# Fewer routed slots, and the high and low halves of the activations side by side in one matmul

## The chip, the cores and the metric

The kernel runs on one core of a Trainium2 chip. The metric is the device time of one execution in microseconds (us). Five things work side by side: TensorE (PE; its weight loads are PEld in the profile), VectorE (DVE), ScalarE (ACT), GpSimd (POOL) and the DMA queues, here mainly SyncE's (SP). Each engine takes its instructions in the order in which the program issued them to it.

## The reference

Three layers on 1,536 tokens of width 512, all in float32: a linear attention with decay, a dense mixture of 4 experts, and a routed mixture of 8 experts. The change lies in the third:

```python
logits = x @ w_gate                      # 1536 x 8
expert_idx = np.argmax(logits, axis=1)   # one expert per token
gate_w = probs[np.arange(N), expert_idx]
for e in range(8):
    xe = x[expert_idx == e]              # n_e x 512
    h = np.maximum(xe @ w1[e], 0.0)      # 512 x 1024
    out[expert_idx == e] = gate_w[...] * (h @ w2[e])   # 1024 x 512
```

With the reference's inputs the experts get 161, 102, 158, 127, 272, 269, 247 and 200 tokens.

## The kernel before, in words

Every float32 matrix is split into a high part (rounded to float32r by ScalarE) and a low part (the rest, by VectorE). A product is three float32r matmuls into one PSUM accumulator: high weight with high activation, high weight with low activation, low weight with high activation (`mm3`, L330).

The routed layer begins at 613 us of the span. Eight experts run one after the other; each has a fixed number of slots (`CAPS`): expert 0 has its own, the other seven are sorted by their token count on the chip and take `BY_RANK` in the order of `TURNS`. So the turns 0 to 7 have 256, 288, 128, 288, 256, 256, 256 and 128 slots. Tokens beyond a capacity would go through a slow loop at the end (`tc.If`, L1014), which does not run with these inputs.

One expert has two products. The first (`moe2_mm1`, L859) makes the hidden layer in 8 groups f of 128 rows, each a PSUM accumulator `g` of 128 x slots over 4 chunks d; ScalarE takes the relu into the high part, VectorE makes the low part (`relu_split`, L339). The second comes in two forms. With at most 256 slots (`moe2_mm2_rows`, L901) the hidden activations are the stationary operand and 512 columns of the weights stream past them: 48 matmuls of 512 columns for 256 slots. With 288 slots (`moe2_mm2`, L930) the weights are stationary and the slots stream: 4 groups m, an eviction `yt`, and transposes back (`moe2_out`, L943). A turn of 128 slots uses the row form for both products. The last step multiplies by the gate and scatters rows to the output.

Between the matmul groups stand hooks (L970 to L990), and through these the order of work on ScalarE and VectorE is set. `hook1`, after each group of the first product, splits two pieces of the same expert's second weights (`split_to`, L138: a ScalarE cast and a VectorE subtraction of 128 x 512 each; a weight half is 4 pieces, an expert has 16). `hook2`, four times in the second product, transposes the next expert's rows (`rows_T`, L846) and splits the next expert's first weights; after a turn in row form it also splits three pieces of its second weights ahead. The matmul accumulators rotate through three PSUM buffers (`ps_mm`). In expert 0, `route_order` and `route_rest` put small VectorE instructions at the start and into the first `hook2`.

Of the kernel before, what the change touches and what calls it, by code (L numbers as in the profile page):

```python
# [8 lines left out]
F32 = mybir.dt.float32  # L9
F32R = mybir.dt.float32r  # L10
BF16 = mybir.dt.bfloat16
I32 = mybir.dt.int32
AF = mybir.ActivationFunctionType
ALU = mybir.AluOpType
# [4 lines left out]
P = 128  # L19
# [7 lines left out]
KD = DM // P  # L27
# [3 lines left out]
FC = HF // P  # L31
# [1 line left out]

BY_RANK = [288, 288, 256, 256, 256, 128, 128]
TURNS = [0, 5, 1, 2, 3, 4, 6]
CAPS = [256] + [BY_RANK[i] for i in TURNS]
NSS = [-(-c // P) for c in CAPS]
STS = [c // n for c, n in zip(CAPS, NSS)]  # L40
CAP, ST, NS = CAPS[0], STS[0], NSS[0]
MOST, NMOST = max(CAPS), max(NSS)
W = DM + 2
FAR = 1 << 20
OMAX = (N - min(CAPS[0], BY_RANK[0]) + P - 1) // P
# [4 lines left out]
def body(ctx: ExitStack, tc: tile.TileContext, lam, att, dp, w1a, w2a, wg, wgt, w1b, w2b, out):  # L50
    nc = tc.nc
    V, A, G, T, SP = nc.vector, nc.scalar, nc.gpsimd, nc.tensor, nc.sync
# [277 lines left out]
    def mm3(ps, parts, first, last):  # L330

        n = 3 * len(parts)
        i = 0
        for (lh, ll), (rh, rl) in parts:
            for l, r in ((lh, rh), (lh, rl), (ll, rh)):
                T.matmul(ps, l, r, start=first and i == 0, stop=last and i == n - 1)  # L336
                i += 1

    def relu_split(ps, tag, n, nm, pl, bufs, most=None):  # L339
        hh, hl = (  # L340
            pl.tile([P, most or n], F32R, tag=tag + x, name=nm + x, bufs=bufs)[:, :n]
            for x in "hl"
        )
        A.activation(out=hh, in_=ps, func=AF.Relu)  # L344
        V.scalar_tensor_tensor(  # L345
            out=hl, in0=ps, scalar=0.0, in1=hh.bitcast(F32), op0=ALU.max, op1=ALU.subtract
        )
        return hh, hl
# [273 lines left out]
    with tc.manual_schedule():  # L622
# [15 lines left out]
            out=upper, in_=upper, compare_op=ALU.is_ge, fill=1.0, base=0,  # L638
# [150 lines left out]
        y, z = NC - 2, NC - 1  # L789
# [17 lines left out]
        gx = z_ctx.enter_context(pool("gx", 2))  # L807

        def rows_tiles(e):
            return tuple(  # L810
                gx.tile([P, KD, MOST], F32R, tag="xg" + x, name=f"xg{x}{e}")[:, :, :CAPS[e]]
                for x in "hl"
            )

        def rows_split(hi, lo, ps):
            A.copy(out=hi, in_=ps)
# [2 lines left out]
        xg = {0: rows_tiles(0)}  # L819
# [4 lines left out]
        gp = z_ctx.enter_context(pool("gp", 2))  # L824
# [21 lines left out]
        def rows_T(e, s):  # L846
            if e >= E2:
                return
            if s == 0:
                xg[e] = rows_tiles(e)  # L850
            hi, lo = xg[e]
            st = STS[e]
            tr = ps_tr.tile([P, KD, P], F32, tag="tr", name=f"xt{e}_{s}")[:, :, :st]
            for d in range(KD):
                T.transpose(tr[:, d, :], xb_t[e][:st, s, d * P:d * P + P], ident[:st, :st])
            c = slice(s * st, s * st + st)
            rows_split(hi[:, :, c], lo[:, :, c], tr)

        def moe2_mm1(e, f):  # L859
            hi, lo = xg[e]  # L860
            k, c = 2 * (E1 + e) + f // FC, (f % FC) * P
            wh, wl = wt[0, k]
            n = CAPS[e]
            ps = ps_mm.tile([P, 512], F32, tag="mm", name=f"g{e}_{f}")
            mm3(
                ps[:, :n],
                [((wh[:, d, c:c + P], wl[:, d, c:c + P]), (hi[:, d, :], lo[:, d, :]))
                 for d in range(KD)],
                True, True,
            )  # L870
            return relu_split(ps[:, :n], "g", n, f"g{e}_{f}", gp, 2 * FC + 2, MOST)


        def moe2_mm1_rows(e, h, hook):
            hi, lo = xg[e]
            wh, wl = wt[0, 2 * (E1 + e) + h]
            n = CAPS[e]
            ps = ps_mm.tile([P, 512], F32, tag="mm", name=f"gr{e}_{h}")
            for d in range(KD):
                mm3(ps[:n], [((hi[:, d, :], lo[:, d, :]), (wh[:, d, :], wl[:, d, :]))],  # L880
                    d == 0, d == KD - 1)
                if d < KD - 1:
                    hook(h * KD + d)
            g = gp.tile([P, HF], F32, tag="gr", name=f"gr{e}_{h}")
            A.activation(out=g[:n], in_=ps[:n], func=AF.Relu)
            hook(h * KD + KD - 1)
            return g
# [13 lines left out]
        def moe2_mm2_rows(e, hs, y, hook):  # L901
            st, ns, xb = STS[e], NSS[e], xb_t[e]
            step = FC * ns // 2
            ps = [
                ps_mm.tile([P, 512], F32, tag="mm", name=f"zr{e}_{s}") for s in range(ns)
            ]
            i = 0
            for h in range(2):
                wh, wl = wt[1, 2 * (E1 + e) + h]
                for s in range(ns):  # L910
                    for f in range(FC):
                        hh, hl = hs[h * FC + f]
                        c = slice(s * st, s * st + st)
                        mm3(ps[s][:st], [((hh[:, c], hl[:, c]), (wh[:, f, :], wl[:, f, :]))],
                            h == 0 and f == 0, h == 1 and f == FC - 1)
                        i += 1
                        if i % step == 0 and i < 4 * step:
                            hook(i // step - 1)
                    if h == 0:
                        continue  # L920
                    gate = xb[:st, s, DM:DM + 1]
                    V.tensor_scalar(  # L922
                        out=y[:st, s, :], in0=ps[s][:st], scalar1=gate, scalar2=None,
                        op0=ALU.mult,
                    )
                    scatter(out, xb.bitcast(I32)[:st, s, DM + 1:W], y[:st, s, :], N, "out")
            hook(3)


        def moe2_mm2(e, hs, m):  # L930
            n = CAPS[e]
            ps = ps_mm.tile([P, 512], F32, tag="mm", name=f"z{e}_{m}")
            c = slice(m * P, m * P + P)
            parts = []
            for f, (hh, hl) in enumerate(hs):
                wh, wl = wt[1, 2 * (E1 + e) + f // FC]
                parts.append(((wh[:, f % FC, c], wl[:, f % FC, c]), (hh, hl)))
            mm3(ps[:, :n], parts, True, True)
            yt = gp.tile([P, MOST], F32, tag="yt", name=f"yt{e}_{m}", bufs=3)
            A.copy(out=yt[:, :n], in_=ps[:, :n])  # L940
            return yt

        def moe2_out(e, yt, m, y):  # L943
# [19 lines left out]
        for e in range(E2):  # L963
            k = 2 * (E1 + e)
            load_rows(e + 2)
            y = gp.tile([P, NMOST, DM], F32, tag="y", name=f"y{e}")
            hs = []
            turns = []

            def hook1(i):  # L970
                if late:
                    late.pop()()
                split_to(1, k + 1, 2)
                if i == KD + 1 and turns:
                    hs.extend(turns.pop()())

            def hook2(i):
                if turns:
                    hs.extend(turns.pop()())
                if late:  # L980
                    late.pop()()
                if e == 0 and i == 0:
                    route_rest()
                if e + 1 < E2:
                    if i < NSS[e + 1]:
                        rows_T(e + 1, i)
                    if CAPS[e] <= 2 * P and i > 1:
                        split_to(1, k + 2, 3)
                    else:
                        split_to(0, k + 3, 2 if i == 0 else 3)  # L990

            if CAPS[e] <= P:
                for h in range(2):
                    g = moe2_mm1_rows(e, h, hook1)
                    turns.append(lambda h=h, g=g: moe2_turn(e, h, g))
            else:
                for f in range(2 * FC):
                    hs.append(moe2_mm1(e, f))
                    hook1(f)
            if CAPS[e] <= 2 * P:  # L1000
                moe2_mm2_rows(e, hs, y, hook2)
            else:
                for m in range(KD):
                    yt = moe2_mm2(e, hs, m)
                    hook2(m)
                    late.append(lambda e=e, yt=yt, m=m, y=y: moe2_out(e, yt, m, y))
# [7 lines left out]
    with tc.If(n_r > 0):  # L1014
        with pool("op", 1) as op:
# [12 lines left out]
                out=upto, in0=tiles_e, scalar1=float(P), scalar2=None, op0=ALU.mult  # L1028
            )
            V.tensor_copy(out=base, in_=upto)  # L1030
            for e in range(1, E2):
                V.tensor_tensor(
                    out=upto[:, e:e + 1], in0=upto[:, e:e + 1], in1=upto[:, e - 1:e], op=ALU.add
# [4 lines left out]
                out=pick, in0=desc.unsqueeze(1).to_broadcast([P, NC, E2]),  # L1038
                in1=m2_all.unsqueeze(2).to_broadcast([P, NC, E2]), op=ALU.is_equal,
            )  # L1040
            V.tensor_tensor(
                out=own_t, in0=pick, in1=base.unsqueeze(1).to_broadcast([P, NC, E2]), op=ALU.mult
# [129 lines left out]
```

## Time and profile before

| | |
|---|---|
| time, median of 3 runs | 797.97 us (796.89 to 798.29) |
| the profiled execution's own time | 797.57 us |
| its span, first to last instruction | 795.6 us |
| granted TensorE clock, mean | 0.996 |
| busy share of the span: PE, PEld, DVE, ACT, POOL | 98%, 82%, 46%, 27%, 15% |
| routed layer | from about 613 us on |

The profiled execution is 0.40 us below the median, and its span 2.0 us below its time. A busy share is an average over stages: VectorE's tenths in the slices of the page go from 2 in the dense layer to 7 in the routed one.

### The profile page before, as it was taken

Reading aid. Unit: us, or ns where it says so; the run is one execution under the profiler, and the core shown is the slowest. Engines: PE = TensorE matmul, PEld = TensorE weight load, DVE = VectorE, ACT = ScalarE, POOL = GpSimd, SP = SyncE. Lnnn points to the kernel's source line nnn. Section 1 sums busy time; section 2 is a strip of 40 time slices with the busy share of each in tenths; the row PEclk is TensorE's granted clock in tenths of the full one; section 3 lists DMA queues with packets and bytes.
Section 4 is the critical chain, followed back from the end, with each engine's and each line's share of the span. In section 5 each row is a group of like instructions: output and inputs, shape, how many; then the busy total and the mean of one; then the engine's idle time right before and its main releaser. Section 6 shows DMA issues by size and latency. Waiting matters only on the chain. (4 is left out here: it accounts for less than half of the span.)

```text
span 795.6 us, 11255 instructions
## 1 busy us (share of the span) xinstructions
PE 778.1 (98%) x4472; PEld 651.5 (82%) x4472; DVE 365.1 (46%) x800; ACT 217.4 (27%) x438; POOL 116.4 (15%) x117
## 2 busy tenths in 40 slices
PE   7899999999999999999999999999999999999996
PEld 6787778888888888888888888878898898998884
DVE  5443321332322232233223233588886757677553
ACT  3222222110121221111022121011134546555552
POOL 4553200100110110001011010011122013121101
PEclk9999999999999999999999999999999999999999
DMA  8654264110010001011001002000123767766550
GB/s 304 228 165 155 80 228 144 53 54 1 26 54 28 26 27 54 0 54 47 7 27 54 26 27 80 0 27 14 41 80 134 280 206 240 277 210 219 176 200 28
DMA packets 24375, 81.20 MB, mean 102 GB/s; under 512 B 3132, under 2 KB 4156, under 8 KB 24192
## 3 DMA queue, kind: packets, MB, share of 16 engines
q1 hardware_dynamic: 22032, 74.14, 27.6%
q0 software_dynamic: 2144, 6.31, 2.0%
q8 instruction: 36, 0.59, 0.3%
q14 instruction: 19, 0.16, 0.1%
q10 hardware_dynamic: 144, 0.01, 0.0%
HBM read 69.40 MB, written 11.70 MB: 102 GB/s over the span
## 5 line engine op out<-in xcount | busy, mean ns | idle before, releaser
L336 PE MATMUL h<-xh,w0h 128*128 128x512 f32 (+1 forms) x432 | 162.9, 377 | 1.1 <-ACT xh L298 1.1
L336 PE MATMUL h<-xl,w0h 128*128 128x512 f32 (+1 forms) x432 | 159.3, 369 | 0.9 <-DVE xl L299 0.8
L336 PE MATMUL h<-xh,w0l 128*128 128x512 f32 (+1 forms) x432 | 159.5, 369 | 0.0
L378 DVE SCALAR_TENSOR_TENSOR acc<-y,p_sb,acc 128x512 f32<-128x512 f32 x84 | 63.1, 751 | 124.6 <-PE y L336 122.8
L336 PEld LDWEIGHTS h<-xh,w0h 128*128 128x128 f32 x432 | 81.2, 188 | 17.1 <-ACT xh L298 1.8
L336 PEld LDWEIGHTS h<-xl,w0h 128*128 128x128 f32 x432 | 81.2, 188 | 17.0 <-DVE xl L299 2.1
L336 PEld LDWEIGHTS h<-xh,w0l 128*128 128x128 f32 x432 | 81.1, 188 | 16.0
L344 ACT ACTIVATE ht_0h<-h 128x512 fp32r<-128x512 f32 (+1 forms) x27 | 14.9, 551 | 246.4 <-PE h L336 246.4
L161 POOL TENSOR_TENSOR w0l<-raw,w0h 128x512 fp32r<-128x512 f32 x17 | 22.3, 1316 | 251.6 <-ACT w0h L159 251.6
L159 ACT CAST w0h<-raw 128x512 fp32r<-128x512 f32 x96 | 53.9, 619 | 7.3 <-DMA raw<-in_w1a 7.3
L336 PE MATMUL g<-xgl,w0h 128*128 128x256 f32 (+1 forms) x192 | 55.0, 287 | 0.4 <-DVE xgl L817 0.4
L336 PE MATMUL g<-xgh,w0h 128*128 128x256 f32 (+1 forms) x192 | 54.9, 286 | 0.2 <-issue 0.2
L336 PE MATMUL g<-xgh,w0l 128*128 128x256 f32 (+1 forms) x192 | 55.1, 287 | 0.0
L159 ACT CAST w1h<-raw 128x512 fp32r<-128x512 f32 x96 | 54.3, 618 | 1.5 <-PE zr L336 1.5
L161 DVE TENSOR_TENSOR w1l<-raw,w1h 128x512 fp32r<-128x512 f32 x80 | 52.5, 694 | 0.3 <-ACT w1h L159 0.3
L161 DVE TENSOR_TENSOR w0l<-raw,w0h 128x512 fp32r<-128x512 f32 x79 | 51.2, 691 | 0.4
L96 POOL DMA_INDIRECT out<-y,xb x16 | 24.6, 1540 | 152.2 <-DVE y L922 75.8
L345 DVE SCALAR_TENSOR_TENSOR ht_0l<-h,ht_0h 128x512 fp32r<-128x512 f32 (+1 forms) x27 | 17.1, 632 | 60.1 <-ACT ht_0h L344 60.1
L336 PE MATMUL y<-w1h,ht_0h 128*128 128x512 f32 x96 | 39.4, 410 | 0.0
L430 DVE CUSTOM_DVE_ANT_0 jl<-acc,wgb 128x512 f32<-128x512 f32 x56 | 38.4, 685 | 0.8
L336 PE MATMUL y<-w1h,ht_3h 128*128 128x512 f32 x96 | 38.2, 397 | 0.0
L336 PE MATMUL y<-w1h,ht_1l 128*128 128x512 f32 x96 | 38.1, 397 | 0.0
(283 smaller groups left out, 1431.0 us busy)
## 6 DMA issues: line engine op xcount, KB each, us to landing
raw<-in_w1b SPq DMA_DIRECT2D x32, 512.0 KB, 6.8
raw<-in_w2b SPq DMA_DIRECT2D x32, 512.0 KB, 3.2
att<-in_att SPq DMA_DIRECT2D x24, 512.0 KB, 4.3
raw<-in_w1a SPq DMA_DIRECT2D x16, 512.0 KB, 7.6
raw<-in_w2a SPq DMA_DIRECT2D x16, 512.0 KB, 3.9
bins<-fill SPq DMA_DIRECT2D x1, 4626.0 KB, 21.7
xb<-bins SPq DMA_DIRECT2D x4, 514.0 KB, 6.3
wgb<-in_wgt SPq DMA_DIRECT2D x1, 2048.0 KB
```

The lines of the kernel that those rows point to most:

```text
L96: i = G.indirect_dma_start(out=dst, out_offset=bass.IndirectOffsetOnAxis(ap=idx, axis=0), in_=src, in_offset=None, bounds_check=rows - 1, ...
L159: A.copy(out=hi, in_=t)
L161: (G if i < 3 else V if i >= 4 * ROUTED else los[i % 2]).tensor_tensor(out=lo, in0=t, in1=hi.bitcast(F32), op=ALU.subtract)
L336: T.matmul(ps, l, r, start=first and i == 0, stop=last and i == n - 1)
L344: A.activation(out=hh, in_=ps, func=AF.Relu)
L345: V.scalar_tensor_tensor(out=hl, in0=ps, scalar=0.0, in1=hh.bitcast(F32), op0=ALU.max, op1=ALU.subtract)
L378: V.scalar_tensor_tensor(out=acc[:, t, 0:DM], in0=ps, scalar=p_sb[:, t, e:e + 1], in1=acc[:, t, 0:DM], op0=ALU.mult, op1=ALU.add,)
L430: V.tensor_tensor_reduce(out=jl, in0=acc[:, t, 0:DM], in1=rt["wgb"][:, e, :], scale=1.0, scalar=0.0, op0=ALU.mult, op1=ALU.add, accum_out= ...
```

## The change

The capacities of the turns become 176, 288, 128, 288, 256, 208, 160 and 128, 1,632 slots in all for 1,856. A turn whose capacity is a multiple of 128 keeps the row form (turns 2, 4, 7). A turn between 128 and 256 slots is now "wide" (turns 0, 5 and 6): high and low activations lie side by side in one tile, one matmul of the high weight takes both (2n columns, for n slots), and one of the low weight takes the high half (n columns). The accumulator then has two halves; ScalarE copies the second to SBUF, VectorE adds the first to it, and relu, low part and transposes read the sum in SBUF. Wide turns use the weights-stationary form for the second product too. In the row form the gate multiplication moves from VectorE to ScalarE.

```diff
-BY_RANK = [288, 288, 256, 256, 256, 128, 128]
+BY_RANK = [288, 288, 256, 208, 160, 128, 128]
-CAPS = [256] + [BY_RANK[i] for i in TURNS]
+CAPS = [176] + [BY_RANK[i] for i in TURNS]
+BY_ROWS = [c % P == 0 for c in CAPS]
+WIDE = [P < c < 2 * P for c in CAPS]
...
         def rows_tiles(e):
-            return tuple(
-                gx.tile([P, KD, MOST], F32R, tag="xg" + x, name=f"xg{x}{e}")[:, :, :CAPS[e]]
-                for x in "hl"
-            )
+            n = CAPS[e]
+            both = gx.tile([P, KD, 2 * MOST], F32R, tag="xg", name=f"xg{e}")[:, :, :2 * n]
+            return both[:, :, :n], both[:, :, n:], both
...
+        def product(e, ps, parts):
+            n = CAPS[e]
+            if not WIDE[e]:
+                mm3(ps[:, :n], [(w, x[:2]) for w, x in parts], True, True)
+                return ps[:, :n]
+            for i, ((wh, wl), (hi, _, both)) in enumerate(parts):
+                T.matmul(ps[:, :2 * n], wh, both, start=i == 0, stop=False)
+                T.matmul(ps[:, :n], wl, hi, start=False, stop=i == len(parts) - 1)
+            s = gp.tile([P, MOST], F32, tag="yt", name=f"s{ps.name}", bufs=4)[:, :n]
+            A.copy(out=s, in_=ps[:, n:2 * n])
+            V.tensor_tensor(out=s, in0=ps[:, :n], in1=s, op=ALU.add)
+            return s
...
         def moe2_mm1(e, f):
...
-            return relu_split(ps[:, :n], "g", n, f"g{e}_{f}", gp, 2 * FC + 2, MOST)
+            g = gp.tile([P, 2 * MOST], F32R, tag="g", name=f"g{e}_{f}", bufs=2 * FC + 2)
+            hh, hl = g[:, :n], g[:, n:2 * n]
+            A.activation(out=hh, in_=s, func=AF.Relu)
+            V.scalar_tensor_tensor(
+                out=hl, in0=s, scalar=0.0, in1=hh.bitcast(F32), op0=ALU.max,
+                op1=ALU.subtract,
+            )
+            return hh, hl, g[:, :2 * n]
...
         def moe2_mm2_rows(e, hs, y, hook):
-                    V.tensor_scalar(
-                        out=y[:st, s, :], in0=ps[s][:st], scalar1=gate, scalar2=None,
-                        op0=ALU.mult,
-                    )
+                    A.activation(out=y[:st, s, :], in_=ps[s][:st], func=AF.Copy, scale=gate)
...
         def moe2_mm2(e, hs, m):
-            mm3(ps[:, :n], parts, True, True)
-            yt = gp.tile([P, MOST], F32, tag="yt", name=f"yt{e}_{m}", bufs=3)
-            A.copy(out=yt[:, :n], in_=ps[:, :n])
+            s = product(e, ps, parts)
+            if WIDE[e]:
+                return s
+            yt = gp.tile([P, MOST], F32, tag="yt", name=f"yt{e}_{m}", bufs=4)
+            A.copy(out=yt[:, :n], in_=s)
...
-                    if CAPS[e] <= 2 * P and i > 1:
+                    if BY_ROWS[e] and i > 1:
                         split_to(1, k + 2, 3)
...
-            if CAPS[e] <= 2 * P:
+            if BY_ROWS[e]:
                 moe2_mm2_rows(e, hs, y, hook2)
```

## Rows read from the trace of the kernel before

**Rows 1.** The page, busy time of each engine over the span.

```profile
PE 778.1 (98%) x4472; PEld 651.5 (82%) x4472; DVE 365.1 (46%) x800; ACT 217.4 (27%) x438; POOL 116.4 (15%) x117
```

**Rows 2.** Busy time by stretch: first product of turn 0; turns 0, 5, 6.

```profile
core 0: us, PE busy (x) PEld busy (x) DVE busy (x) ACT busy (x) POOL busy (x), PEclk, DMA share, GB/s
613.00:624.40 11.40, 11.40 (x96) 11.40 (x97) 9.70 (x26) 7.08 (x17) 0.00 (x0) 1.00 0.70 230
...
613.00:636.70 23.70, 23.70 (x156) 21.45 (x157) 17.96 (x46) 13.64 (x31) 0.00 (x0) 1.00 0.70 247
...
729.20:752.60 23.40, 23.40 (x154) 21.20 (x153) 15.42 (x29) 12.54 (x26) 2.20 (x2) 1.00 0.59 213
752.60:775.50 22.90, 22.90 (x149) 20.77 (x148) 14.93 (x28) 12.48 (x26) 3.16 (x3) 1.00 0.59 202
```

**Rows 3.** Timeline of PE: start us, us, instruction, count, idle before.

```profile
607.57 0.96 PE L451 MATMUL lg<-wg_sb,xt 128*128 128x8 f32 x8
608.38 0.38 PE L616 MATMUL warm_rt<-ones 128*128 128x128 bf16 x4
...
624.49 0.39 PE L336 MATMUL zr<-w1h,g_0h 128*128 128x512 f32 x1
...
627.04 0.40 PE L336 MATMUL zr<-w1h,g_3l 128*128 128x512 f32 x1
...
656.17 0.49 PE L947 MATMUL yo<-ident,yt 128*96 128x128 f32 x3
656.42 0.38 PE L336 MATMUL z<-g_0h,w1h 128*128 128x288 f32 x1
```

**Rows 4.** Timeline of ACT and DVE, first product of turn 0.

```profile
616.41 1.13 ACT L159 CAST w1h<-raw 128x512 fp32r<-128x512 f32 x2
...
621.83 0.39 ACT L344 ACTIVATE g_5h<-g 128x256 fp32r<-128x256 f32 x1 [1.04 <-PE g L336]
...
617.07 0.42 DVE L345 SCALAR_TENSOR_TENSOR g_1l<-g,g_1h 128x256 fp32r<-128x256 f32 x1
617.41 1.28 DVE L161 TENSOR_TENSOR w1l<-raw,w1h 128x512 fp32r<-128x512 f32 x2
618.61 0.42 DVE L345 SCALAR_TENSOR_TENSOR g_2l<-g,g_2h 128x256 fp32r<-128x256 f32 x1
...
622.25 0.42 DVE L345 SCALAR_TENSOR_TENSOR g_5l<-g,g_5h 128x256 fp32r<-128x256 f32 x1 [0.16 <-ACT g_5h L344]
```

**Rows 5.** Timeline of DVE and ACT: a hand-over from DVE to ACT.

```profile
609.79 0.22 DVE L465 TENSOR_SCALAR df<-lg,mx 128x8 f32<-128x8 f32 x1
...
610.10 0.21 ACT L484 ACTIVATE ex<-df 128x8 f32<-128x8 f32 x1 [2.44 <-DVE df L465]
```

**Rows 6.** Groups by line and shape, ACT and DVE: count, busy us, mean ns.

```profile
L159 ACT CAST w1h<-raw 128x512 fp32r<-128x512 f32 x56 | 31.4, 618 | 1.5 <-PE zr L336 1.5
...
L816 ACT CAST xgh<-xt 128x512 fp32r<-128x512 f32 x8 | 4.7, 587 | 12.1 <-PE xt L855 12.1
...
L161 DVE TENSOR_TENSOR w1l<-raw,w1h 128x512 fp32r<-128x512 f32 x64 | 40.5, 681 | 0.0
...
L817 DVE TENSOR_TENSOR xgl<-xt,xgh 128x512 fp32r<-128x512 f32 x8 | 5.5, 692 | 18.8 <-ACT xgh L816 18.8
```

**Rows 7.** Timeline of DVE: end of `route_order`, start and end of `route_rest`.

```profile
615.44 0.17 DVE L586 TENSOR_SCALAR nth<-who 128x7 int32<-128x7 f32 x1
...
625.44 0.20 DVE L594 TENSOR_TENSOR tmp<-place,places 128x49 f32<-128x49 f32 x1
...
627.11 0.16 DVE L611 CAST tiles_n<-count 128x1 int32<-128x1 f32 x1
```

**Rows 8.** Busy time by stretch, with the granted clock (PEclk), columns as in Rows 2.

```profile
5.00:10.00 5.00, 3.28 (x44) 2.65 (x46) 4.39 (x12) 0.23 (x1) 0.00 (x0) 1.00 1.03 370
10.00:15.00 5.00, 4.23 (x36) 3.20 (x32) 2.49 (x5) 3.02 (x6) 4.12 (x4) 0.66 1.03 383
...
608.00:610.00 2.00, 0.84 (x12) 0.71 (x12) 1.83 (x11) 0.00 (x0) 1.26 (x2) 1.00 0.00 0
```

More of the change, by code (lines that the diff above doesn't have):

```diff
@@ L337, in mm3, with relu_split @@
                 i += 1
-    def relu_split(ps, tag, n, nm, pl, bufs, most=None):
+    def relu_split(ps, tag, n, nm, pl, bufs):
         hh, hl = (
-            pl.tile([P, most or n], F32R, tag=tag + x, name=nm + x, bufs=bufs)[:, :n]
+            pl.tile([P, n], F32R, tag=tag + x, name=nm + x, bufs=bufs)
             for x in "hl"
@@ L850, in rows_T @@
                 xg[e] = rows_tiles(e)
-            hi, lo = xg[e]
+            hi, lo, _ = xg[e]
             st = STS[e]
@@ L857, in rows_T @@
             rows_split(hi[:, :, c], lo[:, :, c], tr)
+        def product(e, ps, parts):
[10 more added lines that the diff above has]
+            return s
         def moe2_mm1(e, f):
-            hi, lo = xg[e]
+            hi, lo, both = xg[e]
             k, c = 2 * (E1 + e) + f // FC, (f % FC) * P
@@ L864, in moe2_mm1 @@
             ps = ps_mm.tile([P, 512], F32, tag="mm", name=f"g{e}_{f}")
[L865 to L869, printed above, removed]
+            s = product(e, ps, [
+                ((wh[:, d, c:c + P], wl[:, d, c:c + P]),
+                 (hi[:, d, :], lo[:, d, :], both[:, d, :])) for d in range(KD)
+            ])
+            g = gp.tile([P, 2 * MOST], F32R, tag="g", name=f"g{e}_{f}", bufs=2 * FC + 2)
[4 more added lines that the diff above has]
+                op1=ALU.subtract,
             )
-            return relu_split(ps[:, :n], "g", n, f"g{e}_{f}", gp, 2 * FC + 2, MOST)
+            return hh, hl, g[:, :2 * n]
         def moe2_mm1_rows(e, h, hook):
-            hi, lo = xg[e]
+            hi, lo, _ = xg[e]
             wh, wl = wt[0, 2 * (E1 + e) + h]
@@ L911, in moe2_mm2_rows @@
                     for f in range(FC):
-                        hh, hl = hs[h * FC + f]
+                        hh, hl = hs[h * FC + f][:2]
                         c = slice(s * st, s * st + st)
@@ L934, in moe2_mm2 @@
             parts = []
-            for f, (hh, hl) in enumerate(hs):
+            for f, h in enumerate(hs):
                 wh, wl = wt[1, 2 * (E1 + e) + f // FC]
-                parts.append(((wh[:, f % FC, c], wl[:, f % FC, c]), (hh, hl)))
-            mm3(ps[:, :n], parts, True, True)
-            yt = gp.tile([P, MOST], F32, tag="yt", name=f"yt{e}_{m}", bufs=3)
-            A.copy(out=yt[:, :n], in_=ps[:, :n])
+                parts.append(((wh[:, f % FC, c], wl[:, f % FC, c]), h))
+            s = product(e, ps, parts)
[3 more added lines that the diff above has]
+            A.copy(out=yt[:, :n], in_=s)
             return yt
```

## The prediction

> **What bounds the kernel now.** First the page: TensorE is busy 98% of the span, no other engine half as much [rows 1]. The change lies in the routed layer, so the stretches of that layer come next. In turn 0 the first product has 96 matmuls of 256 columns in 11.40 us, 0.119 us each, and TensorE and its weight loads are both busy all the time; VectorE has 9.70 us of work there and ScalarE 7.08 [rows 2]. So TensorE sets the pace, but VectorE stands close behind. The timelines show how an eviction goes: relu on ScalarE ends at 621.83 + 0.39 = 622.22, VectorE's low part starts at 622.25 [rows 4], and nothing goes back. The last view to keep is VectorE's rhythm where two weight pieces follow each group: low parts start at 617.07 and 618.61, 1.54 us apart, against 11.40/8 = 1.43 us per group on TensorE [rows 2, 4]. Today this lag is absorbed, since only the first four of the eight groups carry pieces.
>
> **What TensorE saves.** 48 matmuls of 512 columns: 624.49 to 627.04 is 11 steps, 0.232 us each [rows 3]. Between 256 and 512 columns that is 0.441 ns a column, so 320, 352 and 416 columns cost 0.147, 0.161 and 0.190 us. A float32r matmul of 160 to 208 columns is not in the trace. Its lower end is 0.232 us scaled by columns, 0.073 to 0.094; its upper end the 0.119 of 256 columns. The eight gate matmuls stream only 8 columns behind full weight loads and start 0.81/8 = 0.101 us apart [rows 3]; I take that, as a weight load alone must cost about as much. A pair is then 0.262 us for 176 slots, 0.291 for 208, 0.248 for 160; a group of four pairs (first product) 1.05, 1.16, 0.99 us; of eight pairs (second product) 2.10, 2.33, 1.98. New are eight transposes back a turn: three take 0.25 us [rows 3], two 0.17, of which three pairs lie inside a turn, 0.5 us. If TensorE alone counted, turn 0 would fall from 23.7 us to 64 x 0.262 plus 1.2 (what the present 23.7 leaves after 11.4 and 48 x 0.232: row transposes, joins) plus 0.5 = 18.5 us.
>
> **What the eviction now costs.** Per group there were two steps, ScalarE then VectorE. Now there are four: ScalarE copies, VectorE adds, ScalarE takes the relu, VectorE the low part, and both engines keep program order, so VectorE stands still between add and low part. Prices: VectorE's two-operand step is 0.42 us at 256 columns [rows 4] and 0.692 at 512 [rows 6], so 0.34 at 176, 0.37 at 208, 0.32 at 160, and the next one starts 0.08 before its end (617.41 against 617.49). ScalarE from PSUM is 0.39 at 256 [rows 4] and 0.587 at 512 [rows 6], so 0.33 at 176, 0.35 and 0.32; from SBUF I add the 0.618 - 0.587 = 0.03 [rows 6], for the relu now reads SBUF; the next starts 0.10 earlier than its end. The hand-over to VectorE is 0.03 [rows 4]; that to ScalarE is at most 0.09 (610.01 to 610.10 [rows 5]) and at least, I assume, the same 0.03; I take 0.06, halfway. The add itself is not in the trace; I price it as the low part, which has the same two operands, with 0.08 either way.
>
> [...]
>
> From one add to the next, with no weight pieces, 176 slots: 0.34 + 0.06 + 0.36 + 0.03 + 0.26 = 1.05 us, just TensorE's pace. With two pieces: the relu starts 0.40 after the add, the first cast 0.66, it ends at 1.28 (0.618), its subtraction starts at 1.31, the second 0.60 later [rows 4], the next add at 2.51. So 2.5 us a group against TensorE's 1.05. For 208 slots 2.56 (one piece 1.96, none 1.13), for 160 slots 2.48 and 1.00. An accumulator is free after its add, so with three of them group f + 3 waits for add f.
>
> **Turn 0**, from a start that lies 0.5 us earlier (612.5: the selections, the placing matmuls and the first evictions are 176 columns wide and no longer 256; 16 x 0.018 plus some 0.2 of VectorE and ScalarE). VectorE is busy with `route_order` until 615.6 [rows 7], now 615.1: add 0. Eight pieces follow groups 0 to 3, so add 4 is at 615.1 + 4 x 2.5 = 625.1, TensorE begins group 7 at 625.5 and ends the first product at 626.55: 14.05 us, not 11.4. Low part 7 is ready at 625.1 + 3 x 1.05 + 1.1 = 629.3; only then can the second product's first accumulator be finished, 629.6. Three groups of 2.1, 1.2 and 0.5 lead to 637.6. That is 25.1 us for 23.7: +1.4.
>
> **Turn 1** waits for VectorE. After 630.4 it has, before the third part of turn 1's columns, three adds (0.8), `route_rest` (625.44 to 627.27, 1.85 [rows 7]), three low parts of rows (1.5), five subtractions (3.0) and two gate multiplications (0.7): 638.3 instead of 637.6, and 0.5 more at the next transposes, which wait for add 3. +1.3.
>
> **Turn 5** (208) follows a row turn that has split three pieces ahead. Those and the gate step, now ScalarE's, put add 0 at 2.9 us (0.43 to the eviction, 0.5, three casts 1.56, copy 0.35). Add 3 is 2.56 + 2.56 + 1.96 later, at 10.0; groups 6 and 7 end at 12.8; low part 7 is ready at 15.7, the first accumulator done at 16.0, then 3 x 2.33 + 0.8 + 0.5 = 24.3 us for 23.4 [rows 2]: +0.9.
>
> **Turn 6** (160) has eight pieces again, because a wide turn before it splits none ahead. Add 0 at 1.7, add 4 at 11.6, first product 13.0, first accumulator 16.0, then 3 x 1.98 + 0.4 + 0.5 = 22.8 for 22.9 [rows 2]: -0.1.
>
> **Turn 7** meets the same late VectorE as turn 1, which today it does not: +1.2. Turns 2, 3 and 4 stay. At the end ScalarE's gate step is 0.15 shorter than VectorE's.
>
> Sum: -0.5 + 1.4 + 1.3 + 0.9 - 0.1 + 1.2 - 0.15 = +4.05 us. On the profiled execution's 797.57 that is 801.6, and with its distance of 0.4 to the median 802.0. Its own bounds: hand-overs of 0.03 or 0.09 give +3 or +5; the add 0.08 shorter or longer, over 36 evictions, -2.5 or +2.5; the narrow matmul at its ends -0.1 or +0.6, since TensorE waits anyway. The forecast alone is 800 to 806.
>
> What I cost at nothing: the weight loads. Each turn still needs 4.2 MB, the queue runs 6 loads of 0.5 MB ahead, and 213 to 247 GB/s over turns 0 and 5 [rows 2] suffice today; turns do not get shorter here, so no more is asked. If they did (18.5 us), it would be 4.7 MB with the rows, 254 GB/s, about today's rate. The wider tiles take the room of the two they replace.
>
> **The rivals.**
>
> A, faster: the exchange hides. If VectorE never waited in it, a group with two pieces would take its own work alone, 0.26 + 0.26 + 1.20 = 1.72 us. Then turns 0, 5 and 6 gain 3.1, 1.9 and 3.0, and the lag that turns 1 and 7 inherit (2.5) goes: 4.05 - 10.5 = -6.5, 791.5 us. For it speaks that four groups of each first product carry no pieces, so that lag can be made up; against it that ScalarE's relu is ordered behind the add and ahead of the casts. It decides from 2.2 us a group: there the sum is zero. In the extreme, TensorE alone counts: 18.5 us for turn 0, 19.9 and 16.8 for turns 5 and 6, 782 us. VectorE's own 8 x 0.52 + 8 x 0.60 = 9.0 us against TensorE's 8.4 in the first product excludes most of that. [...] I give it 0.04 of A's chance.
>
> B, the narrow matmul is dear. At twice 0.232 us scaled, 0.145 to 0.19 us each, TensorE's group comes to 1.2 to 1.5 us and its second product sets more of the time: about +7, 805 us. Nothing in the trace shows a float32r matmul so narrow.
>
> [...]
>
> D, a capacity is exceeded. The counts fit (127 tokens for 128 slots, 158 for 160 are the tightest); one more would start the slow loop, with four loads of 1 MB. 1 in 100.
>
> **How the numbers follow.** The forecast 0.54; A 0.21; B, C and D 0.10 together; between A and the forecast, within 0.2% (1.6 us, about what a measurement can tell from no change), 0.15. Slower 0.64, same 0.15, faster 0.21. The range 793 to 809 leaves out A's lower half, 0.10, and the worst of B and C, 0.07.
>
> **What would show it.** Right: TensorE idle some 1.4 us before groups 4 to 7 of turns 0 and 6, ended by VectorE's add; adds 2.5 us apart while pieces are split and 1.05 after; first products of 13 to 14 us; turn 1's first matmul waiting for its columns. Wrong: adds under 2.2 us apart, or first products under 11.4 us. [...]

## The result and the profile after

| | before | changed |
|---|---|---|
| time, median of 6 runs | 797.19 us | 805.18 us (802.58 to 807.66) |
| ratio, with 95% interval | | 1.0098 [1.008, 1.0116] |
| profiled execution, span | 797.57, 795.6 us | 805.12, 803.3 us |
| granted clock, mean | 0.996 | 0.984 |

The change makes the kernel 8 us slower; the forecast was 4 us slower (802.0, range 793 to 809). The six runs differ more than those of before, and with their clock: the fastest, 802.58 us, had 0.992, the slowest, 807.66, had 0.982.

The page's lines for busy time and clock (answer to [rows 1]):

```profile
PE 778.1 (97%) x4448; PEld 654.7 (81%) x4448; DVE 371.4 (46%) x838; ACT 227.4 (28%) x478; POOL 120.6 (15%) x117
...
PEclk9999999999999999999999999999998899999988
```

There are fewer slots, yet TensorE is busy as long as before. The clock line says where to look: it dips twice in the routed layer, which had no such dip before. By the start of each turn's first matmul in the timeline of TensorE, in us:

| | forecast | before | changed | difference |
|---|---|---|---|---|
| start of turn 0 | -0.5 | 612.98 | 613.71 | +0.7 |
| turn 0 | +1.4 | 23.7 | 26.3 | +2.5 |
| turn 1 | +1.3 | 26.7 | 27.9 | +1.2 |
| turns 2, 3, 4 | 0 | 65.75 | 65.95 | +0.2 |
| turn 5 | +0.9 | 23.4 | 24.7 | +1.3 |
| turn 6 | -0.1 | 22.95 | 23.7 | +0.8 |
| turn 7, to its last matmul | +1.2 | 11.9 | 12.9 | +1.0 |

These make 7.7 us, the difference of the spans. One execution's start of turn 0 also moves with what lies before it: with the full clock at the entry it was 612.0 us in one kept trace (e2_order) and 613.13 in another (e3_clock). The changed kernel's busy time in the same turns (answer to [rows 2]; columns as there):

```profile
613.70:640.00 26.30, 24.11 (x149) 23.38 (x148) 19.55 (x55) 15.56 (x40) 0.00 (x0) 0.81 0.56 192
...
733.80:758.50 24.70, 21.59 (x144) 20.31 (x142) 17.63 (x39) 15.54 (x38) 1.19 (x2) 1.00 0.57 198
758.50:782.20 23.70, 21.11 (x142) 20.29 (x140) 17.29 (x41) 14.48 (x37) 3.33 (x2) 0.86 0.58 186
```

TensorE now has gaps in all three wide turns, and in turns 0 and 6 its clock is at 0.81 and 0.86 on average. What ends its gaps stands in its timeline:

```profile
621.78 0.43 PE L868 MATMUL g<-xg,w0h 128*128 128x352 f32 x1 [0.90 <-DVE sg L872]
622.05 0.24 PE L869 MATMUL g<-xg,w0l 128*128 128x176 f32 x1
622.13 0.35 PE L868 MATMUL g<-xg,w0h 128*128 128x352 f32 x1
...
622.40 0.35 PE L868 MATMUL g<-xg,w0h 128*128 128x352 f32 x1
...
626.72 0.66 PE L868 MATMUL g<-xg,w0h 128*128 128x352 f32 x1
...
628.85 0.56 PE L868 MATMUL z<-g,w1h 128*128 128x352 f32 x1
...
642.30 0.42 PE L967 MATMUL yo<-ident,sz 128*88 128x128 f32 x2 [0.33 <-DVE sz L872]
...
742.55 0.46 PE L868 MATMUL g<-xg,w0h 128*128 128x416 f32 x1 [1.08 <-DVE sg L872]
...
765.41 0.41 PE L868 MATMUL g<-xg,w0h 128*128 128x320 f32 x1 [1.18 <-DVE sg L872]
```

`sg`, line 872, is the add. The long waits stand before groups 5 and 6 in turns 0 and 6 (4 and 5 in turn 5), not before each of groups 4 to 7 as the forecast's sign had it. A pair of 352 and 176 columns takes 622.40 - 622.13 = 0.27 us (0.262 forecast). The eviction in the timelines of DVE and ACT (answer to [rows 4]):

```profile
618.92 0.34 DVE L872 TENSOR_TENSOR sg<-g,sg 128x176 f32<-128x176 f32 x1
619.67 0.34 DVE L888 SCALAR_TENSOR_TENSOR g<-sg,g 128x176 fp32r<-128x176 f32 x1 [0.42 <-ACT g L887]
620.18 1.29 DVE L165 TENSOR_TENSOR w1l<-raw,w1h 128x512 fp32r<-128x512 f32 x2 [0.17 <-ACT w1h L163]
621.39 0.33 DVE L872 TENSOR_TENSOR sg<-g,sg 128x176 f32<-128x176 f32 x1
...
626.33 0.33 DVE L872 TENSOR_TENSOR sg<-g,sg 128x176 f32<-128x176 f32 x1
...
627.34 0.33 DVE L872 TENSOR_TENSOR sg<-g,sg 128x176 f32<-128x176 f32 x1
628.09 0.34 DVE L888 SCALAR_TENSOR_TENSOR g<-sg,g 128x176 fp32r<-128x176 f32 x1 [0.42 <-ACT g L887]
628.35 0.33 DVE L872 TENSOR_TENSOR sg<-g,sg 128x176 f32<-128x176 f32 x1
...
619.29 0.35 ACT L887 ACTIVATE g<-sg 128x176 fp32r<-128x176 f32 x1 [0.89 <-DVE sg L872]
```

Add to add with two pieces: 621.39 - 618.92 = 2.47 us; without: 1.01. VectorE stands 0.42 us between add and low part and 0.17 before the first subtraction; ScalarE waits 0.89 for the add. And the clock by stretch (answer to [rows 8]):

```profile
610.00:617.00 7.00, 7.00 (x34) 6.89 (x32) 4.26 (x22) 1.73 (x7) 0.97 (x1) 0.51 0.34 115
617.00:624.00 7.00, 5.21 (x37) 4.79 (x36) 5.47 (x12) 4.57 (x12) 0.00 (x0) 0.98 0.85 250
624.00:630.40 6.40, 6.00 (x23) 5.70 (x23) 4.11 (x12) 3.67 (x11) 0.00 (x0) 0.50 0.90 365
...
767.00:774.00 7.00, 5.91 (x23) 5.65 (x24) 4.75 (x13) 3.55 (x11) 0.00 (x0) 0.51 0.71 246
```

In three stretches of some 7 us the granted clock was 0.50 to 0.51 (half clock below). One lies at the entry, where the placing matmuls took 0.214 us each: 613.41 - 610.41 is 14 steps. They began 0.43 us earlier than before and ended later, so the start of turn 0 loses its time in them. The two others begin in the first products of turns 0 and 6, after the waits had begun. The placing matmuls in the changed kernel, and the first of them before:

```profile
610.10 0.52 PE L558 MATMUL px<-sel,ah 128*128 128x176 f32 x1
610.41 0.42 PE L558 MATMUL px<-sel,al 128*128 128x176 f32 x1
...
613.41 0.41 PE L558 MATMUL px<-sel,al 128*128 128x176 f32 x1
...
610.53 0.39 PE L554 MATMUL px<-sel,ah 128*128 128x256 f32 x1
```

### The profile page after: what moved, and what is told of

Its sections match the earlier page's. It is cut to its first block, busy times and chain, and to the rows that moved or that the text cites. A ratio compares the mean times of both kernels' runs of the same rounds, so it can differ in the third digit from the quotient of the medians.

```text
span 803.3 us, 11286 instructions
## 1 busy us (share of the span) xinstructions
PE 778.1 (97%) x4448; PEld 654.7 (81%) x4448; DVE 371.4 (46%) x838; ACT 227.4 (28%) x478; POOL 120.6 (15%) x117
## 4 chain that ended last, share of the span: by engine, by line
PE 83%; issue 5%; DVE 5%; DMA 2%; ACT 2%; POOL 1%; SPq 0%; POOLq 0%; ACTq 0%; DVEq 0%
PE h L340 33%; PE y L340 33%; PE g L340 4%; PE z L340 3%; DVE w1l L165 2%; PE zr L340 2%; PE qk L238 1%; PE xo L297 1%; PE xo L291 1%; DVE w0l L165 1%; DMA raw<-in_w1a 1%; ACT w1h L163 1%; PE z L868 1%; DMA xe<-bins 1%; DMA raw<-in_w1b 1%
## 5 line engine op out<-in xcount | busy, mean ns | idle before, releaser
L100 POOL DMA_INDIRECT out<-y,xb x16 | 29.4, 1841 | 155.6 <-DVE y L969 94.2
L868 PE MATMUL g<-xg,w0h 128*128 128x352 f32 (+2 forms) x96 | 33.9, 415 | 7.4 <-DVE sg L872 7.3
L340 PE MATMUL g<-xg,w0h 128*128 128x288 f32 (+1 forms) x192 | 38.0, 292 | 0.4 <-DVE xg L820 0.4
L165 POOL TENSOR_TENSOR w1l<-raw,w1h 128x512 fp32r<-128x512 f32 x16 | 21.1, 1322 | 114.7 <-ACT w1h L163 114.7
```

What stands on the lines that cost most here:

```text
L100: i = G.indirect_dma_start(out=dst, out_offset=bass.IndirectOffsetOnAxis(ap=idx, axis=0), in_=src, in_offset=None, bounds_check=rows - 1, ...
L165: (G if i < 3 else V if i >= 4 * ROUTED else los[i % 2]).tensor_tensor(out=lo, in0=t, in1=hi.bitcast(F32), op=ALU.subtract)
L868: T.matmul(ps[:, :2 * n], wh, both, start=i == 0, stop=False)
```

## The experiments

Two theories were to be told apart and sized: the exchange between ScalarE and VectorE, in program order, holds the wide turns; and TensorE's clock, 0.50 to 0.51 in the three stretches above, adds the rest. Rivals: the work that the added copies and adds bring; narrow matmuls. Each line of the table is a median and the ratio to the kernel before in the same comparison, with its 95% interval; the ratio is taken over the runs and is not exactly that of the two medians.

| | time, us | ratio |
|---|---|---|
| e1_plain: three narrow matmuls, two-step eviction | 819.73 | 1.0274 [1.0257, 1.0291] |
| e2_order: weight pieces between add and relu | 792.95 | 0.9954 [0.9937, 0.9971] |
| e3_clock: TensorE kept busy at the entry and in the waits | 801.25 | 1.0046 [1.0033, 1.006] |
| e4_wide256: wide turns with the old capacities | 817.26 | 1.0243 [1.0228, 1.0259] |
| e5_plain_up: e1 with TensorE kept busy at the entry | 796.05 | 0.9984 [0.9975, 0.9994] |
| e6_even: e2, one piece a group, busy at the entry | 789.19 | 0.99 [0.9884, 0.9917] |
| e7_order_up: e2, busy at the entry | 793.3 | 0.995 [0.9933, 0.9966] |
| e8_up: the changed kernel, busy at the entry | 803.38 | 1.0088 [1.0067, 1.0109] |

**e2_order.** The same instructions in another order.

```diff
-                    hs.append(moe2_mm1(e, f))
-                    hook1(f)
+                    hs.append(moe2_mm1(e, f, hook1))
...
             hh, hl = g[:, :n], g[:, n:2 * n]
+            if WIDE[e]:
+                hook(f)
             A.activation(out=hh, in_=s, func=AF.Relu)
```

(Turns that are not wide call the hook after the low part, as before.)

> The changed kernel with one order turned round: in a wide turn the two weight pieces come between the add and the relu, no longer behind the low part. The same instructions, the same data. Theory (VectorE's and ScalarE's waits for each other in program order are the cost): a group with two pieces takes VectorE's own work, 1.72 us instead of 2.47, first products of turns 0 and 6 fall by about 3 us, turn 5 by 1.9, 797 in all (8 less). Rival (it is the amount of work that the added copies and adds bring): adds stay 2.4 to 2.5 us apart, 804 to 806.

It is 12.2 us faster than the changed kernel and 4.7 faster than the kernel before (797.63 in the same comparison). VectorE's timeline in turn 0:

```profile
616.00 0.33 DVE L872 TENSOR_TENSOR sg<-g,sg 128x176 f32<-128x176 f32 x1
616.25 1.28 DVE L165 TENSOR_TENSOR w1l<-raw,w1h 128x512 fp32r<-128x512 f32 x2
617.46 0.33 DVE L890 SCALAR_TENSOR_TENSOR g<-sg,g 128x176 fp32r<-128x176 f32 x1
617.71 0.33 DVE L872 TENSOR_TENSOR sg<-g,sg 128x176 f32<-128x176 f32 x1
```

VectorE has no wait left here, and add follows add after 1.71 us, its own work. The first products take 10.7, 10.9 and 10.1 us in turns 0, 5 and 6 (15.1, 13.2 and 13.8 in the changed kernel). The copies and adds are all still there, so the rival, their amount of work, falls as the cause of the loss. Some 8 us were expected; the rest is the clock, which stays at 1.00 in turn 0 and at 0.994 over the profiled execution. e3_clock (below), which has the full clock without the new order, is 8.3 us slower than this: that is the order alone, as expected.

**e4_wide256.** The four-step eviction without fewer slots.

```diff
-BY_RANK = [288, 288, 256, 208, 160, 128, 128]
+BY_RANK = [288, 288, 256, 256, 256, 128, 128]
-CAPS = [176] + [BY_RANK[i] for i in TURNS]
+CAPS = [256] + [BY_RANK[i] for i in TURNS]
-BY_ROWS = [c % P == 0 for c in CAPS]
+BY_ROWS = [c == P for c in CAPS]
-WIDE = [P < c < 2 * P for c in CAPS]
+WIDE = [P < c <= 2 * P for c in CAPS]
```

> The capacities of the kernel before, but the turns of 256 slots (0, 4, 5, 6) are wide: TensorE has as much to do as before (0.232 + 0.119 for three of 0.119), only the eviction in four steps and the order of the weight pieces are new. Theory: adds 2.6 us apart while pieces are split, first products of 14.2 us for 11.4, about 3 us a turn and 1.3 each for turns 1 and 7, some 812. Rival (the exchange is harmless, narrow matmuls or the clock are the loss): 797 to 800.

```profile
746.04 0.41 DVE L872 TENSOR_TENSOR sg<-g,sg 128x256 f32<-128x256 f32 x1
746.93 0.43 DVE L888 SCALAR_TENSOR_TENSOR g<-sg,g 128x256 fp32r<-128x256 f32 x1 [0.48 <-ACT g L887]
...
748.65 0.42 DVE L872 TENSOR_TENSOR sg<-g,sg 128x256 f32<-128x256 f32 x1
...
710.00:738.00 28.00, 25.00 (x145) 21.06 (x144) 19.81 (x41) 16.53 (x38) 3.73 (x3) 1.00 0.56 183
738.00:767.00 29.00, 26.15 (x151) 22.07 (x150) 21.04 (x43) 16.68 (x39) 2.15 (x2) 1.00 0.54 175
```

(Timeline of DVE in turn 5, then busy time by stretch, about turns 4 and 5.) The adds are 2.61 us apart, as worked out, at full clock, and the wide form without fewer slots loses 20 us. The edit also gives these turns the other form of the second product. The four turns take 28.6, 28.4, 28.2 and 27.8 us where they took 23.7, 23.8, 23.4 and 22.95. That is nearly 5 us a turn, not 3. The first products, where the exchange with the weight pieces is, take 14.7 to 15.0 us (14.2 expected, 11.4 to 11.8 before) and hold 13 of the 20 us; the second ones take 13.1 to 13.6, where 3 us a turn would leave about 12.3. A pair there takes the 0.35 us assumed, so the rest is waits at the joins and transposes; how much is which was not separated.

**e3_clock and e8_up.** TensorE kept busy. e8 has the second hunk alone.

```diff
+            if WIDE[e] and f > 1:
+                warmup(ps_tr.tile([P, KD, P], F32, tag="tr", name=f"up{e}_{f}")[:, 0, :], 12)
             ps = ps_mm.tile([P, 512], F32, tag="mm", name=f"g{e}_{f}")
...
         route_choose(z)
-        keep_up(4)
+        keep_up(20)
```

> The changed kernel with TensorE kept busy where it waits: 12 small bf16 matmuls ahead of groups 2 to 7 of each wide first product, and 20 instead of 4 ahead of the last selection. Nothing else. Theory (half clock in 610 to 617, 624 to 630 and 767 to 773 us explains what is beyond the forecast of +4): the clock stays at 1.00 there and the time falls by 3 to 4 us, to about 801.5. Rival (TensorE waits for VectorE in those stretches anyway, so its clock is free): under 0.5 us.

> The changed kernel with 20 instead of 4 small matmuls ahead of the last selection, and none in the wide turns: parts e3_clock (801.25) into entry and turns. If the loss lies at the entry (610 to 617 us), about 803; if it lies inside the turns, where TensorE waits for VectorE, nearly nothing is won and 805 stays; e3_clock's 801 would need both.

The clock by stretch, e3_clock:

```profile
610.00:617.00 7.00, 6.86 (x71) 6.67 (x69) 5.30 (x29) 2.75 (x10) 1.75 (x2) 1.00 0.25 85
...
624.00:630.40 6.40, 5.44 (x47) 4.98 (x46) 3.66 (x10) 3.08 (x12) 0.00 (x0) 1.00 0.94 376
...
766.00:774.00 8.00, 7.51 (x70) 7.08 (x67) 4.63 (x13) 4.70 (x15) 0.00 (x0) 1.00 0.49 165
```

and e8_up:

```profile
610.00:617.00 7.00, 6.36 (x49) 6.06 (x47) 5.41 (x22) 2.82 (x9) 0.97 (x1) 1.00 0.37 117
...
624.00:630.40 6.40, 6.26 (x33) 5.95 (x33) 2.78 (x10) 2.59 (x9) 0.00 (x0) 0.65 0.75 301
```

With the full clock in all three places the changed kernel takes 801.25 us, 3.9 less: the clock theory's number, and 0.75 from the forecast that left the clock out. Entry and turns share it: by the medians 1.8 us for the entry (e8_up) and 2.1 from there to e3_clock. The entry's share is less sure, since e8_up's interval overlaps the changed kernel's; the 16 placing matmuls, with 1.91 us (609.67 to 611.58) for the changed kernel's 3.52 (610.10 to 613.62), would account for 1.6.

TensorE does wait for VectorE in the two turns, but the clock there is not free: the last group of the first product comes behind the last long wait. In turn 0 of the changed kernel it took 628.85 - 626.72 = 2.13 us, in e3_clock 626.87 - 625.70 = 1.17. The second product loses nothing by its slow start, and takes 11.1 us in both: at full clock its first accumulator waits 0.51 us for the last low part, at half clock it does not wait. The last group in e3_clock's timeline:

```profile
625.70 0.43 PE L868 MATMUL g<-xg,w0h 128*128 128x352 f32 x1 [0.46 <-DVE sg L872]
...
626.87 0.36 PE L868 MATMUL z<-g,w1h 128*128 128x352 f32 x1
```

**e1_plain and e5_plain_up.** Fewer slots with neither wide matmuls nor their eviction; e5 has `keep_up(20)` as above.

```diff
-WIDE = [P < c < 2 * P for c in CAPS]
+WIDE = [False for c in CAPS]
```

> The new capacities, but no turn is wide: three matmuls of n columns into one accumulator, as in the turns of 288 slots, and an eviction in two steps. Theory (the four-step eviction between ScalarE and VectorE holds the turns): the eviction with two weight pieces falls from 2.47 to about 1.5 us a group, first products follow TensorE again, and the time falls to 779 if a narrow matmul costs the 0.078 us that it takes behind a wide one, to 791 if a weight load holds each at 0.10. Rival (narrow matmuls are what eats the gain): three of them instead of one wide and one narrow cost at least as much, so no faster than the changed kernel, 803 or more.

> Three narrow matmuls and no wide turn, as in e1_plain, with 20 instead of 4 small matmuls ahead of the last selection, so that TensorE enters turn 0 at full clock. In e1_plain turn 0 ran wholly at clock 0.50 (0.213 us for each matmul of 176 columns, 44 us), turns 5 and 6 at 1.00 (0.113 us at 208 and at 160 columns, 22.6 us each). Theory (a float32r matmul costs a weight load, 0.113 us, whatever is under 256 columns, and the loss of e1_plain is the clock of turn 0): turn 0 takes 22 us, the time is about 798, no gain over the kernel before from fewer slots alone. Rival (narrow matmuls pull the clock down by themselves): turn 0 stays at 0.50 and the time near 819.

e1_plain was the miss: 819.73 us, where 779 to 791 were expected. Busy time by stretch, inside turn 0 and turn 5:

```profile
640.00:658.00 18.00, 18.00 (x90) 17.95 (x88) 7.49 (x13) 6.42 (x15) 0.00 (x0) 0.50 0.30 94
...
752.00:775.00 23.00, 23.00 (x211) 23.00 (x209) 14.49 (x29) 13.43 (x31) 1.12 (x2) 1.00 0.64 217
```

Turn 0 ran 44 us at half clock with TensorE busy without a break, and VectorE no longer holds it. At full clock a narrow matmul in such a row cost 0.112 us at 208 columns (turn 5; 96 of them in 10.74 us) and 0.112 at 160 (turn 6; 780.18 to 785.20 is 45 steps), against 0.119 at 256 in the kernel before: from 208 to 160 columns it did not fall. With the clock kept up at the entry, e5_plain_up:

```profile
612.50:634.00 21.50, 21.50 (x196) 21.50 (x197) 16.32 (x46) 12.30 (x30) 0.13 (x1) 1.00 0.75 254
```

Turn 0 takes 23.1 us, its first product 10.79, 0.112 a matmul of 176 columns. The time is 796.05: in the plain form fewer slots win 1.5 us, since three narrow matmuls cost 0.337 and three of 256 cost 0.357. On TensorE the wide form gains more: its pair costs 0.27 (622.13 to 622.40 in the changed kernel). The rival of e1_plain (narrow matmuls eat the gain) holds for the plain form, not for the changed kernel.

**e6_even and e7_order_up.** e2_order with `keep_up(20)`; e6_even moreover:

```diff
-                split_to(1, k + 1, 2)
+                split_to(1, k + 1, 1 if WIDE[e] else 2)
```

> e2_order, with one weight piece after each of the eight groups of a wide turn instead of two after the first four, and 20 instead of 4 small matmuls ahead of the last selection. VectorE then has 0.26 + 0.26 + 0.60 = 1.12 us a group, about TensorE's 1.09 to 1.20. Theory (VectorE's program order sets the first products): they fall from 10.7, 10.9 and 10.1 us to about 9.7, 10.4 and 9.0, the time to 790. Rival (what is left is bound by later waits, for the last low part and in the second product): no change from e2_order, 793.

> e2_order with 20 instead of 4 small matmuls ahead of the last selection, nothing else: parts e6_even into its two edits. e2_order already entered turn 0 at clock 1.00, so 792 to 793; if the entry clock mattered in its unprofiled runs, up to 1 us less.

VectorE in turn 0 of e6_even:

```profile
617.10 0.68 DVE L165 TENSOR_TENSOR w1l<-raw,w1h 128x512 fp32r<-128x512 f32 x1
617.70 0.33 DVE L890 SCALAR_TENSOR_TENSOR g<-sg,g 128x176 fp32r<-128x176 f32 x1
617.95 0.33 DVE L872 TENSOR_TENSOR sg<-g,sg 128x176 f32<-128x176 f32 x1
618.31 0.69 DVE L165 TENSOR_TENSOR w1l<-raw,w1h 128x512 fp32r<-128x512 f32 x1
618.92 0.34 DVE L890 SCALAR_TENSOR_TENSOR g<-sg,g 128x176 fp32r<-128x176 f32 x1
619.17 0.33 DVE L872 TENSOR_TENSOR sg<-g,sg 128x176 f32<-128x176 f32 x1
```

Add to add is 1.2 us, near TensorE's 1.09; the first products take 8.8, 9.85 and 8.4 us, the turns 20.2, 21.5 and 18.5. The 4.1 us between e7 and e6 are the even spread, the only difference of the two; e7 gives nothing over e2, whose profiled execution had the full clock at the entry already. At 789.19 us, 1.0% below the kernel before, e6_even is the fastest version; it keeps the change's saving on TensorE and reorders the eviction and the weight pieces around it.

## Why the prediction was right, and where it was off

- **The exchange, shown.** 2.5 us a group with two pieces and 1.05 without were worked out; 2.47 and 1.01 were measured. In turn 0 add 4 came 12.6 us after the turn's start (626.33 - 613.71) and group 7 began at 13.0, both as worked out. The add, which the trace of before did not have, takes 0.34 us, as its nearest row said. Turning the order round (e2_order) takes the loss away; the wide form without fewer slots (e4_wide256) makes a larger one. e2_order comes near rival A's number (792.95 for 791.5). A's gains in the three wide turns were right, but they need an order that the kernel did not have, and the lag in turns 1 and 7, which A lets go, stays (27.9 and 12.8 us).
- **TensorE's pair.** 0.262 us forecast, 0.27 measured. The parts were wrong and cancelled, which is luck: behind a wide matmul the narrow one costs only 0.08 us (622.05 to 622.13), under the 0.101 taken from the gate matmuls, and the wide one 0.19 (622.13 to 622.32) where 0.161 was worked out. In a row of narrow ones each took 0.112 (e5_plain_up, 176 columns). That a weight load sets such a price was the author's estimate; no run shows it apart.
- **Late VectorE in the next turn.** Turn 1 +1.3 forecast (its terms, 0.7 and 0.5, make 1.2), +1.2 measured; turn 7 +1.2 and +1.0. In turn 1 the transposes wait for VectorE's last add (642.30 above); they come 0.5 us late, as worked out, and the first matmuls some 0.3 us late instead of 0.7. No experiment took this lag away by itself; that the same +1.2 stands in turn 1 of e2_order and e6_even (27.9 us) fits it, as their second products carry the same weight pieces. Not all of it is the adds: in e5_plain_up, which has none, turn 1 is still 0.5 and turn 7 still 0.65 us longer than before.
- **The step that was mis-sized: the clock**, which the sum held at full. Rival C, that the clock falls in the wide turns, had a chance beside the forecast; it came on top of it. The sum said -0.5 us for the start of turn 0, and it was +0.7, because the placing matmuls ran at half clock; turns 0 and 6 came out 1.1 and 0.9 us longer than worked out. In both turns that is group 7 at half clock: 2.13 us in turn 0 and 2.00 in turn 6, where 1.05 and 0.99 were worked out. e3_clock, which restores the clock, gives 801.25 against 802.0. The turns' share is 2.1 us in all (e8_up to e3_clock), and it lies at the end of the first products, not in the second ones. No run of the changed kernel shows a clock that takes the time out of the range, as the chance for the worst of C supposes: entry and turns together made 3.9 us, and the slowest run took 807.66. That the forecast's own bounds (800 to 806) hold 805.18 is luck: they were for hand-overs and the add, which came out as priced, and not for the clock.
- Turn 5, at full clock, came 0.4 us over its sum. Its add 0 came 3.25 us after the turn's start instead of 2.9, directly behind the three subtractions on VectorE, where the sum had counted ScalarE's three casts.
- **B and D** did not happen: narrow matmuls were cheap in the pair (0.08 us at 176 columns), and the slow loop does not appear in the trace. That B's number was 805 too is chance.

What brings the clock down was not settled. Waiting alone does not: in turn 5 of the changed kernel TensorE waits 1.08 us twice, and in turn 0 of e4_wide256 three times for 0.92 to 0.95 us, and the clock stays at 1.00 in both; in turns 0 and 6, with waits of 0.90 to 1.19 us, it falls. e3_clock shows only that keeping TensorE busy there keeps the clock up. At the entry it falls in the changed kernel and not before. TensorE has nearly the same pause in both: 1.16 us before, 0.91 us after the change, both ended by VectorE. In e2_order, with the same instructions at the entry, it did not fall in the profiled execution.

## What to carry to other kernels

When an eviction gains a step on another engine, count the crossings between the two engines and what stands in program order between them, not only the busy time: here the wait for the relu, and what queued behind it, cost 0.76 us a group (2.47 against 1.71), and moving independent work into the gap, with not one instruction fewer, turned a loss of 8 us into a gain of 4.7. Spread such work so that each group gets what the slowest engine can do in that group's time. And where an engine begins to wait, look at TensorE's clock in that stretch before calling the wait harmless.

## What the runs showed of the hardware

- A float32r matmul of 160, 176 or 208 columns in a row of such matmuls cost 0.112 us at full clock (turns 6 and 5 of e1_plain, turn 0 of e5_plain_up); at half clock one of 176 cost 0.213 (turn 0 of e1_plain). Behind a matmul of 352 columns one of 176 cost only 0.08 us, to the start of the next (the changed kernel, 622.05 to 622.13).
- TensorE stayed at half clock (0.50) while it was busy in e1_plain, for the 44 us of turn 0, until the 288 columns of turn 1 had begun; the same matmuls entered at full clock (e5_plain_up, 1.00) stayed there. So here the clock at the start of turn 0 decided over 21 us of it (44.1 against 23.1).
- Waits of 1.08 us between groups left the clock at 1.00 in turn 5 of the changed kernel; with waits of 0.90 to 1.19 us it fell to 0.50 and 0.51 in turns 0 and 6.
- The mean clock of an execution told the spread of its runs: 802.58 us at 0.992, 807.66 at 0.982.
